# Attention and two mixtures on one core: quarter passes over the last keys put ahead of the values' full passes, and transfers of the later stages issued sooner

## The chip, the cores and the metric

One core of one Trainium2 chip runs the whole kernel. The metric is the device time of one launch in microseconds, and the comparison is between medians of runs of the kernel before and of the changed kernel on the same chip.

## The reference

Three layers follow each other; everything is float32. The first is attention over 4 batches, 12 heads, 448 rows and 64 columns, in which the scores are mixed over heads before the softmax and the weights after it. The second is a two-layer perceptron on 1792 tokens of 768 columns. The third is a mixture of 8 experts: a token whose skip score is positive goes through the one expert with the highest logit; the others pass unchanged.

```python
scores = np.einsum('bhij,hg->bgij', q @ k.transpose(0, 1, 3, 2) / 8, w_pre)
attn = softmax(scores)
x = (np.einsum('bhij,hg->bgij', attn, w_post) @ v)  # then 1792 x 768
h = x @ w_in                                        # 768 x 2048
x = np.where(h > 0, h, np.exp(np.minimum(h, 0)) - 1) @ w_out
e = argmax(x @ w_gate); prob = max(softmax(x @ w_gate))
out = x + (x @ w_skip > 0) * prob * (relu(x @ w1[e]) @ w2[e])
```

## The kernel before

**Attention.** The 16 row tiles (four to a batch: 120, 120, 120 and 88 rows) are taken in 48 units, three to a row tile. In the loop over units, TensorE gets for unit n: the mix over heads before the softmax (`mix_pre`, L205, 64x64 tiles), the mix over heads of the softmaxed weights of the unit before (`mix_post`, L265, 64x64 tiles, output `f`), the product with the values of an earlier tile (`av`, output `xp`), the scores of a later tile (`qk`, L164, 64x128 tiles), and the second `mix_post`. The values run over 448 keys as three full passes of 128 keys and a quarter pass of the 64 that remain: L286 are the full passes (twelve matmuls, seen as 24 passes in the trace), L293 the quarter passes (four, seen as eight). All of them accumulate in one PSUM tile: the first full pass opens it, the quarter pass closes it. Values start at unit 4. The scores of a unit belong five units ahead, so they end at unit 42; the last five units have products of the next stage between their parts. ScalarE and VectorE take the row maximum, the exponential and the copies out of PSUM, POOL makes the mixing matrices `kr`.

**Hidden products.** `products(s)` (L626) is the first matmul of the perceptron: 64 groups of 18 matmuls, 16 chunks of hidden columns times 4 batches. Weights arrive as 64-bit floats on SP's queue and are narrowed and split into two parts (high and low), and the activated result goes to DRAM as `gT`. `w_jobs` issues the loads and splits of one chunk. After the eighth group, `tables()` loads the router's weights (gate and skip, `wgt`, L583 and L584), turns the gate's columns on TensorE (`pt`, L589) and writes them as rows `wg` to DRAM. Up to the end of `tables` the order of instructions is as written; after it a scheduler orders each engine's instructions by due times. The second weight's chunks 0 to 8 are kept on chip, and 9 to 15 go to DRAM as `wf`.

**Second stage.** Fourteen row tiles of 128 tokens, 96 matmuls each (L899, output `o`): `load_g` reads `gT` back (`gr`) and splits it (`gh`), four quarters a tile. The seven chunks of `wf` are reloaded (`wr`, L845) through `raw0`, a pool of three buffers, and split into `w`; behind the last of them SP loads the router's rows for all partitions (`wrow`, L849, 3.46 MB). Each row tile is then scored on VectorE (L789, `junk`, nine to a tile), routed (`route`: maximum, exponential, one-hot `oh`) and seated (`seat`: a running count on TensorE gives each token its slot, which POOL scatters to `slots`). The last row tile's tokens are placed for expert 0 by TensorE (`place_old`).

**Experts.** Eight tiles of up to 128 tokens, and one more for the fullest expert. `load_w` brings weights in 0.79 MB pieces (`w1t`, 15 buffers), `part` splits them into `whi` and `wlo` (L1065, L1067), `gather` (L1072) fetches an expert's tokens by list from `x2d`, `turn` transposes them (L1082, output `pt`), `expert_first` and `expert_second` multiply. `plan` finds the fullest expert among the later ones; `reorder` (L1028 to L1038) swaps its list with the last expert's, from the table of lists `ids` and the mask `swap`, and writes `ordered`; gathers from expert 3 on use `ordered`. The order of a queue's entries is that in which they are issued, so a gather waits on POOL until its list is there.

Of the kernel before, what the change touches and what calls it, by code (L numbers as in the profile page):

```python
# [8 lines left out]
FP32 = mybir.dt.float32  # L9
# [4 lines left out]
ALU = mybir.AluOpType  # L14
# [4 lines left out]
B, H, S, D = 4, 12, 448, 64  # L19
NT, DM, DFF = B * S, H * D, 2048  # L20
NK = DM // 128
# [57 lines left out]
def attention(tc, q, k, v, w_pre, w_post, xT, mix):  # L79
# [12 lines left out]
    with ExitStack() as ctx, ExitStack() as mixing, ExitStack() as scoring:  # L92
# [181 lines left out]
        def av(T, u, ps=None):  # L274
# [7 lines left out]
            for i in range(2):  # L282
                p = 2 * u + i
                for jc in range(WHOLE):
                    for z in range(2):
                        nc.tensor.matmul(out=ps[i][z * 64:(z + 1) * 64, :n], lhsT=vt[b, p][:, jc * 2 + z, :],  # L286
                                         rhs=att[T][:, jc * H + ORDER.index(2 * p + z), :n], start=(jc == 0), stop=False)
            for i in range(2):
                p = 2 * u + i
                for z in range(2):  # L290
                    half = (z + p) % 2
                    keys = slice(half * JW, (half + 1) * JW)
                    nc.tensor.matmul(out=ps[i][z * 64:(z + 1) * 64, :n], lhsT=vt[b, p][keys, 2 * WHOLE, :],  # L293
                                     rhs=att[T][keys, WHOLE * H + p, :n], start=False, stop=True)
# [181 lines left out]
def mixtures(tc, order, xT, w_in, w_out, w_skip, w_gate, w1, w2, ident, gT, wf, wg, x2d, slots, out):  # L476
# [5 lines left out]
    with ExitStack() as top:  # L482
# [27 lines left out]
        with ExitStack() as ctx:  # L510
# [63 lines left out]
            def tables():  # L574
# [8 lines left out]
                nc.sync.dma_start(out=wgt[:, :, :E], in_=w_gate.rearrange("(k p) e -> p k e", p=128))  # L583
                nc.sync.dma_start(out=wgt[:, :, E], in_=w_skip.rearrange("(k p) -> p k", p=128))  # L584
# [127 lines left out]
            load_x(3)  # L712
            products(2)
# [31 lines left out]
        with ExitStack() as ctx:  # L745
# [47 lines left out]
            def route(i, lg):  # L793
# [3 lines left out]
                nc.vector.max_index(out=ix, in_max=mx, in_values=lg[:, :E])  # L797
                nmx = st_p.tile([128, 1], FP32, tag="nmx", name="nmx")
# [6 lines left out]
                ef = st_p.tile([128, 1], FP32, tag="ef", name="ef")  # L805
                nc.vector.tensor_copy(out=ef, in_=ix[:, 0:1])
                do = st_p.tile([128, 1], FP32, tag="do", name="do")
                nc.vector.tensor_scalar(out=do, in0=lg[:, E:E + 1], scalar1=0.0, scalar2=None, op0=ALU.is_gt)
                oh = st_p.tile([128, E], FP32, tag="oh", name="oh")
                nc.vector.tensor_scalar(out=oh, in0=iota8, scalar1=ef, scalar2=do, op0=ALU.is_equal, op1=ALU.mult)  # L810
# [32 lines left out]
            for fc in range(EARLY, NF):  # L843
                raw = raw0.tile([128, 2 * DM], FP32, tag="w", name="wr")[:, :DM]
                last_wr = nc.sync.dma_start(out=raw, in_=wf[fc - EARLY])  # L845
                wo[fc] = split(raw, ring_a if fc < RA + RB else ring2)
# [41 lines left out]
            for i, n, fc, cs in work:  # L888
# [35 lines left out]
                if fc == NF - 1:  # L924
                    if 0 in cs:
                        x2 = rows[i] = x2_p.tile([128, DM], FP32, tag="x2", name="x2")
                    for c in cs:
                        to, at = x2[:, cols[c]], po[c][:, :cols[c].stop - cols[c].start]
                        nc.scalar.copy(out=to, in_=at)  # L929
                        if last and c == 1:  # L930
                            turned, freed = score_turned(x2, c)
                            place_old(range(2))
                            logits(turned)
                            place_old(range(2, 5))
# [5 lines left out]
            place_old(range(5, NK))  # L940
# [9 lines left out]
        with ExitStack() as ctx:  # L950
# [284 lines left out]
            def jobs(*js):  # L1235

                return lambda *place: [f(*args) for at, f, *args in js if at == place]

            h, ht = new_h(), []
            expert_first([0], [h], jobs(((3, 2), turn_h, h, ht, 0)))  # L1240
            expert_second(0, ht, jobs(((0,), turn_h, h, ht, 1), ((2,), turn_x, 1)))
            h = new_h()
            expert_first([1], [h], jobs(((1, 2), turn_x, 2)))
            reorder()
            xg[3] = gather(ids[3])
# [111 lines left out]
```

## Time and profile before

| | |
|---|---|
| median of 3 runs | 1022.62 us (1020.44 to 1026.99) |
| the profiled execution | 1024.68 us |
| its span | 1022.9 us |
| TensorE busy in the span | 982.5 us (96%), 12226 matmuls |
| VectorE, ScalarE, POOL busy | 725.8, 555.9, 226.8 us |
| moved by DMA | 199.67 MB, mean 195 GB/s |
| mean granted TensorE clock | 0.988 |

Times in the rows are us from the start of the span. PE is the matmul side of TensorE, PEld its weight loads; "busy" of an engine leaves out instructions that only wait, branch or issue transfers. In a timeline a row is a run of like instructions: start, time up to the last one's end, engine, line, operation, output and inputs, shapes, count, and in brackets the idle time ahead of it with what ended it. In the waits, the numbers are the summed idle time, the count and the longest.

### The profile page before, as it was taken

What the parts mean: (1) busy time and instruction counts of PE and PEld (TensorE: products, weight loads), DVE (VectorE), ACT (ScalarE), POOL (GpSimd) and SP (SyncE); (2) the same over time, 40 slices, a digit from 0 to 9 for tenths busy, and PEclk for the clock granted to TensorE, in tenths of its full rate; (3) what the DMA queues carried; (4) which work ended last, traced back from release to release, by engine and by line L of the source; (5) the groups of instructions that cost most, each with busy time, mean ns of one, the idle gap of its engine ahead of it and who ended that gap; (6) DMA issues with size and microseconds to landing.
All of it is one profiled execution on the core that took longest, in us unless ns stands there. A gap on an engine that the chain in (4) does not pass through costs nothing. (4 is left out here: it accounts for less than half of the span.)

```text
span 1022.9 us, 30007 instructions
## 1 busy us (share of the span) xinstructions
PE 982.5 (96%) x12226; PEld 860.5 (84%) x12226; DVE 725.8 (71%) x1458; ACT 555.9 (54%) x1121; POOL 226.8 (22%) x295
## 2 busy tenths in 40 slices
PE   7899999999998899999999999999999999899997
PEld 4577777777766788999999999999999988799987
DVE  5677776777765777666666477777777748999963
ACT  5687787788765654445444462222222116788851
POOL 2233224224223312232332200010101003321002
PEclk9999999999998989999999999999999999999999
DMA  4665665675646565454665489543434396999800
GB/s 157 214 206 158 218 208 149 205 235 131 216 167 204 160 220 166 156 183 151 227 220 192 140 281 301 155 124 93 123 95 123 99 344 237 393 396 398 322 9 34
DMA packets 132297, 199.67 MB, mean 195 GB/s; under 512 B 35476, under 2 KB 99480, under 8 KB 131901
## 3 DMA queue, kind: packets, MB, share of 16 engines
q1 hardware_dynamic: 130013, 191.27, 56.4%
q0 software_dynamic: 2144, 6.46, 1.6%
q8 instruction: 97, 1.59, 0.7%
q14 instruction: 43, 0.35, 0.1%
HBM read 122.47 MB, written 37.65 MB: 157 GB/s over the span
## 5 line engine op out<-in xcount | busy, mean ns | idle before, releaser
L899 PE MATMUL o<-w,gh 128*128 128x384 f32 (+2 forms) x1344 | 239.2, 337 | 1.2 <-DVE w L505 0.8
L899 PEld LDWEIGHTS o<-w,gh 128*128 128x128 f32 x1344 | 231.9, 188 | 4.5 <-DVE w L505 1.4
L626 PE MATMUL h<-xh,w 128*128 128x448 f32 x1152 | 235.4, 367 | 0.0
L626 PEld LDWEIGHTS h<-xh,w 128*128 128x128 f32 x1152 | 217.4, 189 | 17.3 <-issue 0.4
L265 PEld LDWEIGHTS f<-kr,e 64*64 64x64 f32 x5888 | 106.3, 136 | 39.1 <-issue 29.5
L213 DVE TENSOR_REDUCE nmx<-c 128x1 f32<-128x448 f32 x184 | 102.4, 617 | 51.7 <-PE c L205 51.6
L226 ACT ACTIVATE e<-c,nmx 128x448 f32<-128x448 f32 x184 | 114.2, 632 | 23.0 <-DVE nmx L213 22.8
L789 DVE SCALAR_TENSOR_TENSOR junk<-x,wrow 128x768 f32<-128x768 f32 x117 | 111.8, 955 | 18.3 <-ACT x L929 12.8
L246 POOL TENSOR_SCALAR kr<-kpost,rs 128x60 f32<-128x60 f32 x184 | 78.4, 448 | 200.1 <-DVE rs L241 110.2
L1067 DVE TENSOR_TENSOR wlo<-w1t,whi 128x1536 fp32r<-128x1536 f32 x64 | 111.0, 1751 | 14.3 <-ACT whi L1065 14.0
L265 PE MATMUL f<-kr,e 64*64 64x60 f32 (+1 forms) x5888 | 108.4, 219 | 7.3 <-issue 3.5
L541 POOL TENSOR_TENSOR wf<-a,p 128x768 f32<-128x768 f32 x32 | 66.6, 2081 | 187.2 <-DVE p L539 139.5
L1065 ACT CAST whi<-w1t 128x1536 fp32r<-128x1536 f32 x64 | 93.9, 1482 | 20.6 <-PE ph L1094 9.4
L164 PE MATMUL qk<-k,qq 64*120 64x448 f32 (+1 forms) x576 | 82.6, 408 | 8.1 <-ACT k L135 4.5
L774 ACT CAST gh<-gr 128x512 fp32r<-128x512 f32 x56 | 35.0, 624 | 98.7 <-PE o L899 39.1
L205 PE MATMUL c<-d,kpre_low 64*64 64x448 f32 x368 | 83.3, 554 | 3.0 <-ACT s L168 2.8
L205 PE MATMUL c<-d,kpre_up 60*64 60x448 f32 x368 | 81.8, 554 | 0.0
L271 ACT COPY at<-f 128x420 f32<-128x420 f32 (+1 forms) x136 | 65.4, 516 | 28.2 <-PE f L265 27.2
L164 PEld LDWEIGHTS qk<-k,qq 64*120 64x120 f32 (+1 forms) x576 | 52.1, 186 | 27.8 <-issue 4.6
L286 PE MATMUL xp<-at,v 128*64 128x120 f32 (+1 forms) x1152 | 67.5, 266 | 7.3 <-issue 3.9
L168 ACT ACTIVATE s<-qk 120x448 f32<-120x448 f32 (+1 forms) x96 | 51.7, 544 | 35.5 <-PE qk L164 26.4
L169 DVE TENSOR_SCALAR s<-qk 120x448 f32<-120x448 f32 (+1 forms) x96 | 58.3, 621 | 16.1 <-PE qk L164 8.4
(180 smaller groups left out, 1255.7 us busy)
## 6 DMA issues: line engine op xcount, KB each, us to landing
w1t<-in_moe_w_dram SPq DMA_DIRECT2D x64, 768.0 KB
d<-s SPq DMA_DIRECT2D x176, 210.0 KB
gT<-g SPq DMA_DIRECT2D x64, 224.0 KB
f<-in_moe_w_in_dram SPq DMA_DIRECT2D x16, 768.0 KB
f<-in_moe_w_out_dram SPq DMA_DIRECT2D x16, 768.0 KB
gr<-gT SPq DMA_DIRECT2D x48, 256.0 KB
rk<-in_k_dram SPq DMA_DIRECT2D x24, 224.0 KB
v<-in_v_dram SPq DMA_DIRECT2D x24, 224.0 KB
```

Of the source, the lines that this page charges most:

```text
L164: nc.tensor.matmul(out=ps[:n, :S], lhsT=qt[T, p // 2][rows, a, p % 2, :n], rhs=kt[b, p][rows, z, :], start=(i == 0), stop=(i == 2))
L205: nc.tensor.matmul(out=ps[j * UP:(j + 1) * UP, :S], lhsT=kpre_up[UP:UP + HP, :] if z else kpre_low, rhs=d[z, j])
L213: nc.vector.tensor_reduce(out=t, in_=c, op=ALU.max, axis=AX.X, negate=True)
L226: nc.scalar.activation(out=e, in_=c, func=ACTF.Exp, bias=t, accum_out=sms[0][:, k + i:k + i + 1])
L246: nc.gpsimd.tensor_scalar(out=kr, in0=kposts[z], scalar1=rs[:, 2 * i + z:2 * i + z + 1], scalar2=None, op0=ALU.mult)
L265: nc.tensor.matmul(out=ps[to, heads, z, :], lhsT=e[rows, keys * JW:(keys + 1) * JW], rhs=kr[rows, first * HR:(first + n) * HR])
L286: nc.tensor.matmul(out=ps[i][z * 64:(z + 1) * 64, :n], lhsT=vt[b, p][:, jc * 2 + z, :], rhs=att[T][:, jc * H + ORDER.index(2 * p + z), :n] ...
L626: nc.tensor.matmul(out=ps, lhsT=w[:, a, kk, :], rhs=xs[tb, kk][:, z, :], start=(kk == 0 and a + z == 0), stop=(kk == NK - 1 and a == 1))
L789: nc.vector.scalar_tensor_tensor(out=t[:, o:o + n], in0=x2, scalar=1.0, in1=w, op0=ALU.mult, op1=ALU.mult, accum_out=lg[:, e:e + 1])
L899: mm = nc.tensor.matmul(out=po[c][:, :cols[c].stop - cols[c].start], lhsT=gs[i][fc // GC][:, a, fc % GC, :], rhs=wo[fc][:, z, cols[c]], st ...
L1065: nc.scalar.copy(out=hi, in_=t)
L1067: nc.vector.tensor_tensor(out=lo, in0=t, in1=hi, op=ALU.subtract)
```

## The change

1. `av`: the quarter passes come first and open the accumulation, the full passes follow and close it.
2. The two loads of `wgt` move out of `tables` to just behind the load of the fourth batch's `x`.
3. `route`: the cast of the index, the comparison of the skip score and the one-hot `oh` come ahead of the exponential, its sum and the reciprocal.
4. The reloads of `wf` share `raw0`'s buffers by twos: both loads of a pair are issued, then both are split.
5. `place_old` is split 2:4 and 4:6, where it was 2:5 and 5:6.
6. `reorder` and the gather of expert 3 come ahead of the second product of expert 0, where they came behind the first product of expert 1.

```diff
@@ av
-                for jc in range(WHOLE):
-                    for z in range(2):
-                        nc.tensor.matmul(out=ps[i][z * 64:(z + 1) * 64, :n], lhsT=vt[b, p][:, jc * 2 + z, :],
-                                         rhs=att[T][:, jc * H + ORDER.index(2 * p + z), :n], start=(jc == 0), stop=False)
-            for i in range(2):
-                p = 2 * u + i
                 for z in range(2):
                     half = (z + p) % 2
                     keys = slice(half * JW, (half + 1) * JW)
                     nc.tensor.matmul(out=ps[i][z * 64:(z + 1) * 64, :n], lhsT=vt[b, p][keys, 2 * WHOLE, :],
-                                     rhs=att[T][keys, WHOLE * H + p, :n], start=False, stop=True)
+                                     rhs=att[T][keys, WHOLE * H + p, :n], start=True, stop=False)
+            for i in range(2):
+                p = 2 * u + i
+                for jc in range(WHOLE):
+                    for z in range(2):
+                        nc.tensor.matmul(out=ps[i][z * 64:(z + 1) * 64, :n], lhsT=vt[b, p][:, jc * 2 + z, :],
+                                         rhs=att[T][:, jc * H + ORDER.index(2 * p + z), :n], start=False,
+                                         stop=(jc == WHOLE - 1))
@@ tables
-                nc.sync.dma_start(out=wgt[:, :, :E], in_=w_gate.rearrange("(k p) e -> p k e", p=128))
-                nc.sync.dma_start(out=wgt[:, :, E], in_=w_skip.rearrange("(k p) -> p k", p=128))
@@ ahead of products(2)
             load_x(3)
+            nc.sync.dma_start(out=wgt[:, :, :E], in_=w_gate.rearrange("(k p) e -> p k e", p=128))
+            nc.sync.dma_start(out=wgt[:, :, E], in_=w_skip.rearrange("(k p) -> p k", p=128))
             products(2)
@@ route
                 nc.vector.max_index(out=ix, in_max=mx, in_values=lg[:, :E])
+                ef = st_p.tile([128, 1], FP32, tag="ef", name="ef")
+                nc.vector.tensor_copy(out=ef, in_=ix[:, 0:1])
+                do = st_p.tile([128, 1], FP32, tag="do", name="do")
+                nc.vector.tensor_scalar(out=do, in0=lg[:, E:E + 1], scalar1=0.0, scalar2=None, op0=ALU.is_gt)
+                oh = st_p.tile([128, E], FP32, tag="oh", name="oh")
+                nc.vector.tensor_scalar(out=oh, in0=iota8, scalar1=ef, scalar2=do, op0=ALU.is_equal, op1=ALU.mult)
                 nmx = st_p.tile([128, 1], FP32, tag="nmx", name="nmx")
...
                 nc.vector.reciprocal(out=pairs[:, i, 1:2].bitcast(FP32), in_=sm)
-                ef = st_p.tile([128, 1], FP32, tag="ef", name="ef")
-                nc.vector.tensor_copy(out=ef, in_=ix[:, 0:1])
-                do = st_p.tile([128, 1], FP32, tag="do", name="do")
-                nc.vector.tensor_scalar(out=do, in0=lg[:, E:E + 1], scalar1=0.0, scalar2=None, op0=ALU.is_gt)
-                oh = st_p.tile([128, E], FP32, tag="oh", name="oh")
-                nc.vector.tensor_scalar(out=oh, in0=iota8, scalar1=ef, scalar2=do, op0=ALU.is_equal, op1=ALU.mult)
@@ reloads
-            for fc in range(EARLY, NF):
-                raw = raw0.tile([128, 2 * DM], FP32, tag="w", name="wr")[:, :DM]
-                last_wr = nc.sync.dma_start(out=raw, in_=wf[fc - EARLY])
-                wo[fc] = split(raw, ring_a if fc < RA + RB else ring2)
+            for f0 in range(EARLY, NF, 2):
+                raw = raw0.tile([128, 2, DM], FP32, tag="w", name="wr")
+                fcs = range(f0, min(f0 + 2, NF))
+                for fc in fcs:
+                    last_wr = nc.sync.dma_start(out=raw[:, fc - f0], in_=wf[fc - EARLY])
+                for fc in fcs:
+                    wo[fc] = split(raw[:, fc - f0], ring_a if fc < RA + RB else ring2)
@@ last row tile
-                            place_old(range(2, 5))
+                            place_old(range(2, 4))
...
-            place_old(range(5, NK))
+            place_old(range(4, NK))
@@ experts
             expert_first([0], [h], jobs(((3, 2), turn_h, h, ht, 0)))
+            reorder()
+            xg[3] = gather(ids[3])
             expert_second(0, ht, jobs(((0,), turn_h, h, ht, 1), ((2,), turn_x, 1)))
             h = new_h()
             expert_first([1], [h], jobs(((1, 2), turn_x, 2)))
-            reorder()
-            xg[3] = gather(ids[3])
```

On TensorE, a unit of attention stands like this before (`f` is the mix over heads, `xp` the values, `qk` the scores), with the mix ahead and the next mix behind:

```order
L265 MATMUL f<-kr,e 64x12x5 x12
L265 MATMUL f<-kr,e 64x6x5 x4
L286 MATMUL xp<-at,v 64x120 x12
L293 MATMUL xp<-at,v 64x120 x4
L164 MATMUL qk<-k,qq 120x448 x12
L265 MATMUL f<-kr,e 64x12x5 x12
```

and like this in the changed kernel, where L287 are the quarter passes and L293 the full ones:

```order
L265 MATMUL f<-kr,e 64x12x5 x12
L265 MATMUL f<-kr,e 64x6x5 x4
L287 MATMUL xp<-at,v 64x120 x4
L293 MATMUL xp<-at,v 64x120 x12
L164 MATMUL qk<-k,qq 120x448 x12
L265 MATMUL f<-kr,e 64x12x5 x12
```

The four quarter passes now stand between the mix and the twelve full passes; nothing else of the unit moved.

On SP's queue, at the end of the hidden products, the reloads (`wr`), reads of `gT` (`gr`) and the router's rows (`wrow`) stand like this before:

```order
L845 DMA wr<-wf_79 128x768
L771 DMA gr<-gT_0_61 128x4x128
L771 DMA gr<-gT_0_65 128x4x128
L637 DMA gT_3_76<-g 128x448
L771 DMA gr<-gT_0_69 128x4x128
L845 DMA wr<-wf_80 128x768
L771 DMA gr<-gT_0_73 128x4x128
L771 DMA gr<-gT_0_61 128x4x128
L845 DMA wr<-wf_81 128x768
L845 DMA wr<-wf_82 128x768
L845 DMA wr<-wf_83 128x768
L849 DMA wrow<-wg 128x3840
```

and like this in the changed kernel:

```order
L848 DMA wr<-wf_79 128x768
L848 DMA wr<-wf_80 128x768
L636 DMA gT_3_76<-g 128x448
L848 DMA wr<-wf_81 128x768
L848 DMA wr<-wf_82 128x768
L772 DMA gr<-gT_0_61 128x4x128
L772 DMA gr<-gT_0_65 128x4x128
L848 DMA wr<-wf_83 128x768
L853 DMA wrow<-wg 128x3840
L853 DMA wrow<-wg 128x3072
L772 DMA gr<-gT_0_69 128x4x128
L772 DMA gr<-gT_0_73 128x4x128
```

The reloads 80 to 83 moved ahead of reads of `gT` for the second row tile, and the router's rows ahead of two of these reads.

On VectorE, in the same place, the low halves of reloaded weights (`w`), of `gh` and the scorings of the first row tile (`junk`) stand like this before:

```order
L775 TENSOR_TENSOR gh<-gr,gh 128x512 x2
L505 TENSOR_TENSOR w<-wr,w 128x768 x2
L775 TENSOR_TENSOR gh<-gr,gh 128x512
L505 TENSOR_TENSOR w<-wr,w 128x768
L775 TENSOR_TENSOR gh<-gr,gh 128x512
L505 TENSOR_TENSOR w<-wr,w 128x768 x2
L775 TENSOR_TENSOR gh<-gr,gh 128x512
L505 TENSOR_TENSOR w<-wr,w 128x768
L789 SCALAR_TENSOR_TENSOR junk,lg<-x_10298,wrow 128x768 x9
L775 TENSOR_TENSOR gh<-gr,gh 128x512
```

and like this in the changed kernel:

```order
L506 TENSOR_TENSOR w<-wr,w 128x768 x5
L776 TENSOR_TENSOR gh<-gr,gh 128x512 x2
L506 TENSOR_TENSOR w<-wr,w 128x768
L790 SCALAR_TENSOR_TENSOR junk,lg<-x_10295,wrow 128x768 x6
L776 TENSOR_TENSOR gh<-gr,gh 128x512 x2
L790 SCALAR_TENSOR_TENSOR junk,lg<-x_10295,wrow 128x768 x3
L776 TENSOR_TENSOR gh<-gr,gh 128x512 x3
```

The third and fourth quarter of the second row tile's `gh` moved behind six of the first row tile's scorings.

Elsewhere, TensorE's transposes of `wgt` stand behind 126 of the products that follow the first group, where they stood behind 175, and POOL issues two gathers from `ordered` ahead of the first scatter of results, where it issued none.

## Rows read from the trace of the kernel before

**Rows 1.** Windows by stage: engines' busy time (instructions), granted clock, DMA share, GB/s

```profile
50.00:348.00 298.00, 286.63 (x8002) 217.54 (x7996) 208.91 (x471) 228.56 (x607) 93.57 (x187) 0.98 0.61 189
225.00:250.00 25.00, 24.59 (x697) 18.77 (x692) 18.49 (x42) 21.98 (x59) 13.22 (x22) 1.00 0.58 161
362.00:596.00 234.00, 231.81 (x1146) 214.52 (x1147) 155.86 (x224) 112.36 (x185) 61.34 (x30) 0.99 0.55 184
844.00:847.00 3.00, 3.00 (x16) 3.00 (x16) 0.69 (x6) 0.00 (x0) 0.68 (x1) 0.50 0.06 20
920.00:940.00 20.00, 20.00 (x112) 18.20 (x111) 19.57 (x17) 16.42 (x17) 4.58 (x3) 1.00 1.04 398
```

**Rows 2.** Waits of PE over the whole span

```profile
PE pt L1082 <- DMA xg<-x2d,ordered: 3.0, 1, 3.0
...
PE pt L589 <- DMA wgt<-in_moe_w_gate_dram: 2.2, 1, 2.2
```

**Rows 3.** Timeline of PE, one unit of attention (start, duration, instruction)

```profile
150.68 1.08 PE L265 MATMUL f<-kr,e 64*64 64x60 f32 x64
151.69 1.45 PE L286 MATMUL xp<-at,v 128*64 128x120 f32 x24
153.07 0.44 PE L293 MATMUL xp<-at,v 64*64 64x120 f32 x8
153.44 1.48 PE L164 MATMUL qk<-k,qq 64*120 64x448 f32 x12
154.84 1.13 PE L265 MATMUL f<-kr,e 64*64 64x60 f32 x64
155.79 0.57 PE L205 MATMUL c<-d,kpre_low 64*64 64x448 f32 x1
```

**Rows 4.** Timeline of PE, two later units without scores

```profile
345.65 0.43 PE L293 MATMUL xp<-at,v 64*64 64x120 f32 x8
345.90 1.08 PE L265 MATMUL f<-kr,e 64*64 64x60 f32 x64
...
355.26 0.38 PE L293 MATMUL xp<-at,v 64*64 64x88 f32 x8
355.57 1.13 PE L286 MATMUL xp<-at,v 128*64 128x88 f32 x24
```

**Rows 5.** Timeline of PE, hidden products up to the router's transposes

```profile
362.38 37.21 PE L626 MATMUL h<-xh,w 128*128 128x448 f32 x175
...
401.78 0.82 PE L589 MATMUL pt<-ident,wgt 128*8 128x128 f32 x6 [2.19 <-DMA wgt<-in_moe_w_gate_dram]
```

**Rows 6.** Timeline of SP's queue, the fourth batch's x

```profile
370.18 2.77 SPq L552 DMA_DIRECT2D xr<-xT  x6
```

**Rows 7.** Timeline of PE, first row tile of the second stage and after

```profile
596.46 13.77 PE L899 MATMUL o<-w,gh 128*128 128x384 f32 x78
...
611.46 2.01 PE L899 MATMUL o<-w,gh 128*128 128x384 f32 x10 [0.38 <-DVE w L505]
...
614.63 17.67 PE L899 MATMUL o<-w,gh 128*128 128x384 f32 x100 [0.38 <-DVE w L505]
```

**Rows 8.** Timeline of SP's queue, last reloads and the router's rows

```profile
605.87 2.66 SPq L845 DMA_DIRECT2D wr<-wf  x3
608.63 0.85 SPq L849 DMA_DIRECT2D wrow<-wg  x2
```

**Rows 9.** Timeline of DVE, first scoring

```profile
617.55 0.96 DVE L789 SCALAR_TENSOR_TENSOR junk<-x,wrow 128x768 f32<-128x768 f32 x1 [2.98 <-DMA wrow<-wg]
```

**Rows 10.** Timeline of POOL, gather of expert 3

```profile
881.48 2.25 POOL L1072 DMA_INDIRECT xg<-x2d,ordered  x1 [6.36 <-DVE ordered L1035]
```

**Rows 11.** Timeline of DVE, the mask for the swap, and splits of weights

```profile
861.92 0.15 DVE L981 TENSOR_SCALAR swap<-star 128x8 int32<-128x8 f32 x1
...
884.37 3.41 DVE L1067 TENSOR_TENSOR wlo<-w1t,whi 128x1536 fp32r<-128x1536 f32 x2
```

**Rows 12.** Timeline of PE, transposes of expert 3

```profile
889.73 0.30 PE L1082 MATMUL pt<-ident,xg 128*128 128x128 f32 x1 [3.02 <-DMA xg<-x2d,ordered]
```

## The prediction

> **What bounds the kernel now.** The page comes first. TensorE is busy 982.5 us of a span of 1022.9, so the time is TensorE's own work plus its short waits, and an edit elsewhere pays only where TensorE waits for it. The windows by stage [rows 1] say how firm that is: in attention (50 to 348) TensorE is busy 286.63 of 298 us, in the stage of hidden products (362 to 596) 231.81 of 234. Attention leaves little slack beside it: in the stretch where keys are also split (225 to 250) ScalarE works 21.98 of 25 us. In the experts (920 to 940) VectorE works 19.57 of 20 and the DMA engines are full.
>
> The waits of TensorE name what ends its pauses. Two entries are transfers that come late [rows 2]: 3.0 us for the gathered rows of an expert and 2.2 us for the router's weights. Pauses smaller than a microsecond don't show there. For them I read TensorE's timeline: once inside a unit of attention [rows 3, 4], then at the three places that the change touches later [rows 5, 7, 12]. Behind each stood one look at the queue that brings the late data [rows 6, 8, 10] and at VectorE's work beside it [rows 9, 11].
>
> **Part 1: quarter passes lead (attention).** No matmul is added or removed. What changes is which shapes meet. Before, a unit goes mix (64x64 tiles), full passes (128x64), quarter passes (64x64), scores (64x128), mix: three changes of tile shape up to the scores. After it, mix and quarter passes have one shape, so two changes are left, quarter to full and full to scores. What one costs I read from starts [rows 3, 4]. The quarter passes take 153.44 - 153.07 = 0.37 us up to the scores, but 345.90 - 345.65 = 0.25 us up to a mix of their own shape: 0.12 for the change. A mix takes 151.69 - 150.68 = 1.01 us up to full passes and 155.79 - 154.84 = 0.95 up to the 64x64 product after it: 0.06. I take the middle, 0.09. It counts where scores follow the values. Values start at unit 4, and scores are five units ahead, so they end at unit 42: 39 units. 39 x 0.09 = 3.5 us; by the ends 2.3 and 4.7, and 0 if another engine sets the pace. In the other nine units a mix or more values follow: the shapes change as often as before, so nothing there.
>
> The Trainium skill (page "TensorEngine Tiling (Array Packing)", section "Key Properties") says that changing the tiling mode, not merely the tile, drains TensorE; the two start distances above agree. Its page "TensorE: Matmul & The Clock Gate", section "Step-by-step: what each phase is for", gives about 128 cycles for the last column to leave the array, 53 ns at 2.4 GHz; an estimate by that page would be 39 x 0.053 = 2.1 us instead of 3.5.
>
> **Part 2: router weights loaded early.** Before, their six transposes stand behind 175 products, and the data is 2.19 us late [rows 5]. The change issues the load right behind that of the fourth batch's x; that one's six issues end at 370.18 + 2.77 = 372.95 [rows 6]. The transposes now stand behind 126 products, so they want the data at 362.38 + 126 x 37.21/175 = 389.2. That leaves 16 us, so the whole 2.2 goes. SP issues two more transfers ahead of the next weight load, so that one starts about 1 us later (SP spends 2.66/3 = 0.9 us on a wr issue [rows 8]); it is narrowed only when the products of the next chunk are under way, and TensorE has its products queued. Ends: 0 and 2.2.
>
> **Part 3: reloads in pairs.** The first row tile of the second stage waits for reloaded weights. By 614.63 it has done 78 + 2 + 10 + 2 = 92 of its 96 matmuls [rows 7]. At the steady 17.67/100 = 0.1767 us the 92 would have ended at 596.46 + 92 x 0.1767 = 612.72: 1.9 us lost, in pieces that end with VectorE's or ScalarE's split. Three reloads fit in three buffers; in pairs six do, and the seventh waits for two splits. So the whole loss goes. The router rows (wrow), issued at 608.63 behind the last reload [rows 8], come with it some 4 us sooner, and were wanted at 617.55 by the first scoring, which waited 2.98 for them [rows 9].
>
> What is late next: the order on VectorE now puts six scorings ahead of the split of tile 1's third quarter. Tile 0 would end at 612.72 + 4 x 0.1767 = 613.4; about 1.2 later its rows are copied out; six scorings at 0.96 [rows 9] bring 620.4, and the split (0.8) 621.2. TensorE wants it 48 matmuls into tile 1: 613.4 + 48 x 0.1767 = 621.9. Just in time. If the router rows landed no sooner than before, it would be 617.55 + 5.8 + 0.8 = 624.1, 2.2 us late. I take +1.9; ends: -0.3 and +1.9.
>
> **Part 4: the swapped list and its gather sooner.** TensorE waits 3.02 us at expert 3's transposes, up to 889.73 [rows 12]. The gather that it waits for was issued at 881.48, the queue having stood 6.36 us for the list `ordered` [rows 10]: 8.2 us from issue to use. One input of `ordered`, `swap`, was there at 861.92 [rows 11]; the other is the table of lists, whose transfer POOL issues behind the gathers of experts 0 to 2; no row here dates its landing, and I take it to be in by then. After the change the list comes right behind both, near 863, and the gather near 865, landing at about 873, against a want at 889.73 - 3.02 = 886.7. POOL's only other work in the way is the gather itself, now ahead of the first scatter of results, which nobody reads. VectorE meets the small reorder operations ahead of splits of weights; these wait for nothing late if the table has landed. What is late next is a split of weights (1.71 us each): VectorE ends one at 884.37 + 3.41/2 = 886.1 [rows 11], 0.6 before the want, the second at 887.8. If TensorE wants that one within the same microsecond, up to 1.5 us comes back as a wait for it. Ends 1.5 and 3.0; I take 3.0, since the transposes want no weights.
>
> **Part 5: the router's order, and placing 2:4 and 4:6.** Three small VectorE operations move ahead of the exponential, and two of TensorE's placing matmuls move behind the last seat. At the end of the stage TensorE is busy 3.00 of 3.00 us [rows 1], at a granted clock of 0.50, the lower of its two levels (1.2 of 2.4 GHz), after the products thinned out there. A filled stretch has nothing to give: 0, with 0.3 either way.
>
> **Sum.** 3.5 + 2.2 + 1.9 + 3.0 = 10.6. The profiled execution took 1024.68 us (its span and 1.8 around it): 1014.1. It lies 2.06 above the median of the three runs, 1022.62, and inside them (1020.44 to 1026.99). Against the median the sum gives 1012.0.
>
> **Rivals.** *Attention is paced elsewhere.* If ScalarE (21.98 of 25 us) or a fixed chain from mix to copy sets the unit, the 3.5 stay as idle time: 1015.5. For it: ScalarE's share where keys are split. Against: TensorE is busy 24.59 of the same 25.
>
> *The experts are bound by transfers or VectorE.* Then the 3.0 come back as later waits for weights: 1015.0. For it: 398 GB/s and VectorE 19.57 of 20 [rows 1]. Against: TensorE is busy 20.00 of the same 20.
>
> *Tile 1 waits behind the scorings.* Part 3 turns from +1.9 into -0.3: 1014.2.
>
> *Slower: the new meeting costs more than the old.* If going from quarter to full passes, now with the accumulation begun by the small tile, stalled TensorE in all 48 units, it would eat parts 2 to 4 (7.1) from 7.1/48 = 0.15 us per unit, and be over 1% slower from (7.1 + 10.2)/48 = 0.36. At 0.4 it takes 19.2: 1022.6 - 7.1 + 19.2 = 1034.7. Against: at 355.26 quarter passes of one group already meet full ones of the next, 0.31 from start to start [rows 4]; with 88 of 120 columns 0.25 shrinks to 0.18, so that change costs 0.13, no more than the others. For it: there the next accumulators are other ones.
>
> *Nothing arrives:* the waits are replaced one for one, 1022.
>
> **Chances.** Two medians of this kernel differ by chance up to about 1%, 10.2 us; below 1012.4 counts as faster. Forecast (own range 1009 to 1014.5, about three in four of it below 1012.4): 0.56. Attention paced elsewhere 0.17, experts 0.12, tile 1 0.07, all three within 1%; some of the first ends faster if parts 2 to 4 give their ends. Slower 0.04. Nothing 0.04. That makes faster 0.45, same 0.51, slower 0.04. The range: all upper ends (4.7 + 2.2 + 1.9 + 3.0 + 0.3 = 12.1) give 1010.5, less half the runs' spread (3.3) 1007; attention lost, part 3 at its lower end and part 4 at its own leave 2.2 - 0.3 + 1.5 = 3.4, so 1019.2, rounded up to 1020.
>
> **What would show it.** TensorE's timeline in attention: mix to quarter near 0.95, quarter to full near 0.37, full to scores unchanged or 0.05 longer, and the attention stage some 3.5 us shorter. No wait of TensorE for wgt; its transposes at about 386 to 389. Tile 0's 96 matmuls in 17 us and no pause at 48 of tile 1. No wait for xg in the experts, the gather issued before 870. Wrong would be a stage of attention as long as before, a wait of 1 us or more for gh near 620, or new waits for whi or wlo behind 887.

## The result and the profile after

| | before | changed |
|---|---|---|
| median (runs) | 1023.41 us (4: 1020.44 to 1026.99) | 1013.55 us (4: 1006.87 to 1017.75) |
| ratio to before | | 0.9879, 95% interval 0.983 to 0.9929 |
| profiled execution, its span | 1024.68, 1022.9 us | 1017.75, 1016.0 us |
| TensorE busy, mean granted clock | 982.5 us, 0.988 | 978.6 us, 0.984 |

By the medians the change gained 9.9 us, 1.0%; the ratio in the table, 0.9879, is 1.2% or 12.4 us. The forecast was 1012.0, with 10.6 us of gain. The line of 1% at which the chances were drawn runs between the two.

The waits of TensorE in the changed kernel, longest sums first (engine and tile, what it waited for: sum in us, times, longest):

```profile
PE f L265 <- issue: 5.1, 6, 2.0
PE qk L164 <- ACT k L135: 4.9, 1, 4.9
PE f L265 <- DVE at L271: 3.4, 1, 3.4
PE xp L293 <- issue: 3.0, 4, 1.2
PE xp L287 <- DVE x L303: 2.9, 1, 2.9
PE c L205 <- ACT s L168: 2.8, 1, 2.8
```

Both entries of [rows 2], for `xg` and for `wgt`, are gone from the list. What is left stands in attention. A pause that ends with "issue" is one in which TensorE waited for nothing that the profile shows. The windows of the same stretches as [rows 1]:

```profile
50.00:348.00 298.00, 282.87 (x8030) 214.97 (x8024) 208.85 (x472) 228.18 (x606) 94.57 (x189) 0.98 0.61 189
362.00:596.00 234.00, 233.95 (x1163) 216.66 (x1160) 157.50 (x225) 113.17 (x187) 63.09 (x30) 0.99 0.57 186
920.00:940.00 20.00, 20.00 (x110) 18.42 (x109) 18.58 (x16) 16.04 (x15) 3.59 (x2) 1.00 1.04 398
```

The hidden products are now filled (233.95 of 234). Attention is not: TensorE was busy 3.8 us less in the same 298 us, and the stage took no less time. That was the first thing to explain. Cut at three starts of TensorE (first hidden product, first `o`, first `ph`, the hidden product of an expert), the two profiles compare like this:

| stage | before | changed |
|---|---|---|
| start to the first hidden product | 348.66 | 349.27 |
| to the first matmul of the second stage | 247.80 | 245.60 |
| to the first product of expert 0 | 252.45 | 250.06 |
| to the end of the span | 173.99 | 171.07 |

The three later stages give 2.2 + 2.4 + 2.9 = 7.5 us, all that the spans differ by and more. Attention, where 3.5 was forecast, gave -0.6. Yet inside a unit the gain is plain. TensorE's timeline of a unit, to be laid beside [rows 3]:

```profile
140.24 1.08 PE L265 MATMUL f<-kr,e 64*64 64x60 f32 x64
141.14 0.42 PE L287 MATMUL xp<-at,v 64*64 64x120 f32 x8
141.49 1.45 PE L293 MATMUL xp<-at,v 128*64 128x120 f32 x24
142.87 1.44 PE L164 MATMUL qk<-k,qq 64*88 64x448 f32 x12
144.23 1.13 PE L265 MATMUL f<-kr,e 64*64 64x60 f32 x64
```

From the mix to the values it is 0.90 us (1.01 before), quarter to full 0.35 (0.37 before up to the scores), full to scores 1.38 as before. In other units the trace shows the last mixing passes and the first quarter passes interleaved:

```profile
194.79 0.80 PE L265 MATMUL f<-kr,e 64*64 64x60 f32 x41
195.40 0.28 PE L287 MATMUL xp<-at,v 64*64 64x88 f32 x1
195.42 0.27 PE L265 MATMUL f<-kr,e 64*64 64x30 f32 x6
195.51 0.36 PE L287 MATMUL xp<-at,v 64*64 64x88 f32 x7
```

So 0.13 us per unit, 39 x 0.13 = 5.1 us. What hid it in this profile are pauses of TensorE that end with "issue" and stretches at the lower clock level. Between 48 and 300 us the changed kernel's profile has nine such pauses, 8.2 us in all (before: four, 5.1), the longest this one:

```profile
126.75 0.26 PE L265 MATMUL f<-kr,e 64*64 64x30 f32 x5 [1.99 <-issue]
```

Its granted clock fell to 0.50 twice before 300 us (first near 36, then after the pause above), that of before only once, near 294. The columns are those of [rows 1]:

```profile
36.00:38.00 2.00, 1.92 (x9) 1.12 (x13) 1.15 (x2) 1.57 (x5) 0.00 (x0) 0.50 0.85 259
128.00:130.00 2.00, 2.00 (x22) 1.68 (x20) 0.34 (x1) 0.00 (x0) 1.65 (x4) 0.50 0.32 118
```

So the pauses are 3.1 us longer in sum, and the stretches at the lower level some 7 us longer, which at half the clock is up to 3.4 us of time. By this estimate 6.5 us stood against the 5.1, enough for a stage that is 0.6 longer. But one profile of each kernel can't show that it is always so. The experiments had to.

### The profile page after: what moved, and what is told of

It reads as the page before. It is cut to its first block, busy times and chain, and to the rows that moved or that the text cites. A ratio compares the mean times of both kernels' runs of the same rounds, so it can differ in the third digit from the quotient of the medians.

```text
span 1016.0 us, 30002 instructions
## 1 busy us (share of the span) xinstructions
PE 978.6 (96%) x12226; PEld 860.0 (85%) x12226; DVE 724.7 (71%) x1458; ACT 555.6 (55%) x1121; POOL 244.6 (24%) x295
## 5 line engine op out<-in xcount | busy, mean ns | idle before, releaser
L164 PEld LDWEIGHTS qk<-k,qq 64*120 64x120 f32 (+1 forms) x576 | 52.6, 187 | 26.3 <-ACT k L135 4.9
L293 PE MATMUL xp<-at,v 128*64 128x120 f32 (+1 forms) x1152 | 68.8, 268 | 3.0 <-issue 3.0
```

What stands on the lines that cost most here:

```text
L164: nc.tensor.matmul(out=ps[:n, :S], lhsT=qt[T, p // 2][rows, a, p % 2, :n], rhs=kt[b, p][rows, z, :], start=(i == 0), stop=(i == 2))
```

## The experiments

**The order of the values, alone and taken back.** Four kernels on one chip, beside 23 runs of the kernel before (median 1024.06). The first is the changed kernel again.

> The changed kernel once more, with a second profile. Theory: all four terms are there in every execution, so about 9.9 us below the kernel before (ratio 0.990), and the trace shows the same stages after attention as the first profile (hidden products 245.6 us, second stage with the move to the experts 250.1, experts 171.1, each within 0.3). Attention differs from profile to profile: the first one had 8.2 us of pauses of TensorE that end with issue (between 48 and 300 us) and two stretches at the lower clock, the kernel before 5.1 us and one. Rival: the new order of the values itself makes more such pauses; then this profile shows about 8 us again.

Measured: 1012.66 us (6 runs), ratio 0.9887, interval 0.9854 to 0.9921. Attention was 7 us shorter than in the first profile (first hidden product at 342.24), with 4.1 us of pauses before 300 us and no fall of the clock before 316. The later stages took 246.7, 249.2 and 170.7, none of them within the 0.3 that I had expected. So the first profile's attention was one draw among several; the rival on more pauses is taken up below.

In the second kernel only the order in `av` is as before:

```diff
-                                     rhs=att[T][keys, WHOLE * H + p, :n], start=True, stop=False)
-            for i in range(2):
-                p = 2 * u + i
                 for jc in range(WHOLE):
...
+                                         rhs=att[T][:, jc * H + ORDER.index(2 * p + z), :n], start=(jc == 0), stop=False)
+            for i in range(2):
+                p = 2 * u + i
                 for z in range(2):
...
+                                     rhs=att[T][keys, WHOLE * H + p, :n], start=False, stop=True)
```

> The changed kernel with the values' full passes leading again, as before. Theory (a change of tile shape costs TensorE 0.1 us or a little more, nothing else paces attention): 39 units times 0.13 us (start distances of the two profiles) = 5.1 us more than the changed kernel. My own term before the result was 3.5. Rival (attention paced by ScalarE or by the supply of instructions): within 1.5 us of the changed kernel. In the trace: 1.02 us from a mix to the full passes, no mix interleaved with values.

Measured: 1015.51 us (6 runs), ratio 0.9916, interval 0.9886 to 0.9947: 2.9 us above the changed kernel. The two intervals overlap, so these times alone don't exclude the rival. Its trace shows the old distances, 1.03 from mix to values and 0.36 from quarter to scores:

```profile
143.03 1.10 PE L265 MATMUL f<-kr,e 64*64 64x60 f32 x64
144.06 1.45 PE L286 MATMUL xp<-at,v 128*64 128x120 f32 x24
145.44 0.44 PE L293 MATMUL xp<-at,v 64*64 64x120 f32 x8
145.80 1.46 PE L164 MATMUL qk<-k,qq 64*88 64x448 f32 x12
```

Unit by unit against the changed kernel's second profile, the start of the scores comes 0.1 to 0.15 us later with each undisturbed unit; the pauses add or take away 0.4 to 2.4 us at a time. The unit itself is a constant of the order: from the mix to the scores its median is 2.76 us in both profiles with the old one and 2.63 in each of the eleven with the new one. Of the 0.13, 0.11 lies between the mix and the values. The third kernel is the one before with the new order in `av` and nothing else.

> The kernel before with the order of the values alone changed. Theory: 5.1 us faster than before (ratio 0.995), the later stages as before (hidden products 247.8 us with 2.2 us of waiting for the router's weights, experts 174.0). Rival (attention paced elsewhere): within 1.5 us of before.

Measured: 1019.8 us (12 runs), ratio 0.9951, interval 0.9923 to 0.9979: 5.0 us by the ratio, 4.3 by the medians. Hidden products 248.2, experts 175.3, with the old waits for `wgt` (1.86) and `xg`. The interval is 2.1 to 7.9 us of gain, so the order alone makes the kernel faster; the two estimates are 2.9 and 5.0. "Attention paced elsewhere" (within 1.5) falls. The fourth kernel meets more changes of shape:

```diff
                                      rhs=att[T][keys, WHOLE * H + p, :n], start=True, stop=False)
-            for i in range(2):
-                p = 2 * u + i
                 for jc in range(WHOLE):
```

> The changed kernel with quarter and full passes alternating by pair of heads: quarter, full, quarter, full, so four changes of tile shape where it has two up to the scores. The work is the same. Theory (each change costs 0.11 to 0.13 us of TensorE's time): 48 units times 2 more changes times 0.12 = 11.5 us more than the changed kernel, so slower than before by 1 to 2 us. Rival (the gain came from the mix running together with the quarter passes, and the other changes cost nothing): within 2 us of the changed kernel. Rival (attention paced elsewhere): within 2 us as well, with TensorE's pauses smaller.

Measured: 1025.75 us (12 runs), ratio 1.0024, interval 0.9998 to 1.0049: 13.1 above the changed kernel, near the 11.5 that the theory asked for, but by luck: the units grew by twice as much, and about half of it arrived. The unit:

```profile
140.68 0.42 PE L287 MATMUL xp<-at,v 64*64 64x120 f32 x4
141.03 0.84 PE L291 MATMUL xp<-at,v 128*64 128x120 f32 x12
141.79 0.42 PE L287 MATMUL xp<-at,v 64*64 64x120 f32 x4
142.15 0.84 PE L291 MATMUL xp<-at,v 128*64 128x120 f32 x12
142.91 1.44 PE L164 MATMUL qk<-k,qq 64*88 64x448 f32 x12
```

Four quarter passes take the 0.35 us that eight took: for the same columns the two pairs of heads use different halves of the rows, and they had run side by side. A unit's values grew by 0.50 us (2.23 from the first quarter pass to the scores, 1.73 in the changed kernel). The full passes, which this does not touch, give a clean price: 24 in one run took 1.38 us up to the scores, two runs of 12 take 0.76 each, so one change more costs 0.14. The rival in which the other changes cost nothing falls by this reading, not by the time. The other 0.36 is the second group of quarter passes, an estimated 0.25 of passes that no longer run together ([rows 4]: 0.25 without a change of shape) and 0.11 for a change. And 48 x 0.50 = 24 us of longer units came out as 13.1 in the median: some 0.55 of what the units show. For the new order it is 2.9 to 5.0 of 5.1. In this profile the pauses before 300 us sum to 2.6 us, in the two with the old order to 5.1 and 4.0, in the eleven with the new order to 4.1 to 8.2, 5.8 in the mean. One place shows how some of the gain can go. At the 4779th matmul the mix runs through before the change, and it stops in the changed kernel's second profile:

```profile
204.34 1.08 PE L265 MATMUL f<-kr,e 64*64 64x60 f32 x64
```

```profile
200.99 0.59 PE L265 MATMUL f<-kr,e 64*64 64x60 f32 x27
202.55 0.70 PE L265 MATMUL f<-kr,e 64*64 64x30 f32 x33 [0.97 <-issue]
```

It stops there in ten of the eleven profiles with the new order (0.2 to 2.3 us, 1.0 in the mean of all eleven) and in none of the three others; a second place (the 3639th) stops in nine of eleven, 0.4 in the mean, and in none of the three. That shorter units meet longer pauses fits the part that is missing; with three profiles on one side it is not shown.

**The four other parts, each taken back.** On another chip, beside 23 runs of before (median 1022.93). All four are the changed kernel with one part as before. The changed kernel itself did not run beside them, and the interval of each reaches into that of the changed kernel above (0.9854 to 0.9921), so what a part is worth is read from the traces.

```diff
             load_x(3)
-            nc.sync.dma_start(out=wgt[:, :, :E], in_=w_gate.rearrange("(k p) e -> p k e", p=128))
-            nc.sync.dma_start(out=wgt[:, :, E], in_=w_skip.rearrange("(k p) -> p k", p=128))
...
                 nc.sync.dma_start(out=x2d[NT:NT + 1, :], in_=wgs[0:1, :])
+                nc.sync.dma_start(out=wgt[:, :, :E], in_=w_gate.rearrange("(k p) e -> p k e", p=128))
+                nc.sync.dma_start(out=wgt[:, :, E], in_=w_skip.rearrange("(k p) -> p k", p=128))
```

> The changed kernel with the two loads of the router's weights back in the tables. Theory: TensorE's transposes (after 175 products again) wait 2.2 us for the data, and the kernel takes 2.2 us more than the changed one. Rival (the load was hidden by another delay that remains): no wait for wgt, the same time within 1 us.

Measured: 1014.73 us (10 runs), ratio 0.9913, interval 0.9884 to 0.9943. The wait is back, but smaller than before:

```profile
400.40 0.82 PE L590 MATMUL pt<-ident,wgt 128*8 128x128 f32 x6 [0.73 <-DMA wgt<-in_moe_w_gate_dram]
```

Counted from the first hidden product, the data came 0.7 us sooner than in [rows 5] (400.40 - 348.02 = 52.4, there 401.78 - 348.66 = 53.1), and TensorE wanted it 0.7 later (51.7 and 50.9). The expected 2.2 was a miss in size. With the 1.86 of the kernel above, this part is worth 0.7 to 2.2.

```diff
-            for f0 in range(EARLY, NF, 2):
-                raw = raw0.tile([128, 2, DM], FP32, tag="w", name="wr")
...
+            for fc in range(EARLY, NF):
+                raw = raw0.tile([128, 2 * DM], FP32, tag="w", name="wr")[:, :DM]
+                last_wr = nc.sync.dma_start(out=raw, in_=wf[fc - EARLY])
+                wo[fc] = split(raw, ring_a if fc < RA + RB else ring2)
```

> The changed kernel with one reload to a buffer again, three in flight. Theory: four short pauses of TensorE before w in the first row tile, 1.2 us of idle shown and 2.2 us from the first to the 192nd matmul lost against the changed kernel (35.7 us instead of 33.4). Rival (six in flight are not what helps, the earlier router rows are): the first row tile without pauses, and pauses at the second instead. Rival (the loads are sooner anyway because attention ends sooner): nothing lost.

Measured: 1011.95 us (8 runs), ratio 0.9903, interval 0.9872 to 0.9935. In the trace the first row tile stops again for `w`:

```profile
608.28 2.62 PE L900 MATMUL o<-w,gh 128*128 128x384 f32 x12 [0.37 <-DVE w L506]
611.28 17.66 PE L900 MATMUL o<-w,gh 128*128 128x384 f32 x100 [0.37 <-DVE w L506]
```

The two first row tiles took 35.4 us; eleven profiles with reloads in pairs show 33.4 to 34.6. So 0.8 to 2.0 lost, though the timed runs don't show it.

```diff
-            reorder()
-            xg[3] = gather(ids[3])
             expert_second(0, ht, jobs(((0,), turn_h, h, ht, 1), ((2,), turn_x, 1)))
             h = new_h()
             expert_first([1], [h], jobs(((1, 2), turn_x, 2)))
+            reorder()
+            xg[3] = gather(ids[3])
```

> The changed kernel with the reorder and the gather of expert 3 back behind the first product of expert 1. Theory: the gather is issued some 32 us after the seat of the last tile, TensorE waits 3.0 us for it at its first transpose of expert 3, and the experts take 2.9 us more (174.0 instead of 171.1 from the first hidden product of expert 0 to the end). Rival (weights paced the experts anyway): the wait is there, but the time to the end is the same within 0.5 us.

Measured: 1015.29 us (10 runs), ratio 0.9936, interval 0.9905 to 0.9966; the experts took 173.9 us, and the wait of [rows 12] is back whole:

```profile
880.11 0.30 PE L1086 MATMUL pt<-ident,xg 128*128 128x128 f32 x1 [3.26 <-DMA xg<-x2d,ordered]
```

That the weights pace the experts falls: they took 2.8 us longer than in the changed kernel's first profile.

```diff
-                ef = st_p.tile([128, 1], FP32, tag="ef", name="ef")
...
                 nc.vector.reciprocal(out=pairs[:, i, 1:2].bitcast(FP32), in_=sm)
+                ef = st_p.tile([128, 1], FP32, tag="ef", name="ef")
...
-                            place_old(range(2, 4))
+                            place_old(range(2, 5))
```

> The changed kernel with the router's order and the split of the placing matmuls (2:5, 5:6) as before. Theory (this part was worth 0, at most 0.3): from the last six matmuls of the row tiles to expert 0's first product 9.6 us instead of 9.5, total time unchanged within the runs' spread. Rival (this end of the stage is a chain through the one-hot, and its order pays): 0.6 us or more longer.

Measured: 1012.55 us (5 runs), ratio 0.9887, interval 0.9831 to 0.9942. From the last six matmuls of the row tiles (836.55) to expert 0's first product (846.03) it took 9.48 us; in the changed kernel 844.93 - 835.46 = 9.47. Both had the lower clock for some of that time; under it, this part of the change is worth nothing.

**What the profiles offered next.** Two waits of the list above stand at the end of attention in every profile so far: 3.4 us for `at` and 2.9 for `x`. In the changed kernel's timeline of TensorE:

```profile
326.64 0.44 PE L265 MATMUL f<-kr,e 64*64 64x60 f32 x2 [3.38 <-DVE at L271]
...
360.57 0.57 PE L287 MATMUL xp<-at,v 64*64 64x88 f32 x8 [2.91 <-DVE x L303]
```

and the reason for the first, on VectorE, which stands for the first weight's transfer ahead of the next maximum:

```profile
323.30 0.56 DVE L533 TENSOR_SCALAR a<-a 128x768 int32<-128x768 int32 x1 [6.46 <-ACT a L530]
```

Both were moved, together and alone. (a) is the first piece below: a `yield` is a place in attention's units, and the narrowing begins at the sixth instead of the third, with its later steps closed up. (b) is the second.

```diff
             raws[0] = load_w_in(0)
             yield
             yield
             yield
-            step = narrowing(raws.pop(0))
-            next(step)
             yield
             load_x(0)
             yield
-            next(step)
             yield
+            step = narrowing(raws.pop(0))
             next(step)
...
-        next(mix)
         moves = [av(len(tiles) - 1, 0), av(len(tiles) - 1, 1, [ps_f.tile([128, 512], FP32, tag="f", name="xp") for _ in range(2)])]
         moves[0]()
         moves.append(av(len(tiles) - 1, 2))
-        for f in moves[1:]:
-            f()
+        moves[1]()
+        next(mix)
+        moves[2]()
```

> The changed kernel with two more moves, at waits that every profile here shows at the end of attention, with the old order of the values and with the new. (a) The narrowing of the first weight, whose transfer is issued at 314.66 and lands at 322.3, comes two units' parts later, so that ScalarE and VectorE don't stand for it (3.6 and 6.5 us) in front of the next softmax; TensorE waits 3.4 us behind that, and its clock is at the lower level for some 7 us right after. (b) The last values are copied out of PSUM ahead of the splits of the second batch's x; TensorE waits 2.9 us for that copy, and the lower clock follows for some 6 us. No arithmetic is changed. Theory: both waits go (6.3 us), and with them a part of the stretches at the lower clock (up to 3 us each): 6 to 12 us below the changed kernel, 1001 to 1007. Rival (attention's end is bound by the transfer of the weights or by x): the waits move to the first hidden products, and the time stays within 2 us.

> Move (a) alone. Theory: 3.4 us of waiting for `at` and up to 3 us of lower clock behind it go: 3 to 6 us below the changed kernel, and the second wait (2.9 for x) stays. Rival: the first hidden products wait for their weights instead, nothing gained.

> Move (b) alone. Theory: 2.9 us of waiting for x and up to 3 us of lower clock go: 3 to 6 us below the changed kernel, and the first wait (3.2 to 3.7 for `at`) stays. Rival: the products of the second batch wait for their split x instead, nothing gained.

Measured beside 11 runs of before (median 1021.13): both 0.989 (0.9846 to 0.9933), (a) alone 1011.19 us and 0.988 (0.9845 to 0.9916), (b) alone 1013.95 us and 0.9909 (0.9875 to 0.9944). All three lie where the changed kernel lies, so my 6 to 12 us for both is refuted by these runs. (Both ran six times; one execution took 4211.67 us, for a reason that the record does not show, and is not in the ratio.) The waits themselves went; of the first, 0.6 to 1.3 us are left with (a). With both moves, the last values of attention run through (compare the 2.91 above):

```profile
351.84 0.38 PE L287 MATMUL xp<-at,v 64*64 64x88 f32 x8
352.16 1.13 PE L293 MATMUL xp<-at,v 128*64 128x88 f32 x24
353.22 4.18 PE L625 MATMUL h<-xh,w 128*128 128x448 f32 x19
357.65 10.59 PE L625 MATMUL h<-xh,w 128*128 128x448 f32 x50 [0.26 <-DVE xh L561]
```

From the last scores (307.85) to these products it is 45.4 us; the ten profiles without these moves have 52.0 to 54.0, (a) alone 52.6, (b) alone 49.3. To learn whether the timed runs had been unlucky, both moves ran once more.

> Both late moves once more. Its first profile shows the end of attention (last scores to the products of the second batch) in 45.4 us, where ten kernels without the moves show 52.0 to 54.0, yet its timed runs lay no lower than those of the changed kernel (ratio 0.989 as against 0.988 and 0.989). Theory: the 7 us are there in every execution, and the five runs were slow by chance in the stretch before (units 4 to 42 took 254.3 us in its profile, 249.8 to 255.6 in others of the same order): ratio 0.982 to 0.985, tail again 45 to 46.5. Rival (the time comes back behind attention, where the hidden products wait or the clock falls instead): ratio 0.988 to 0.990, and a later stage longer by some 5 us than in the changed kernel.

Measured beside 11 other runs of before (median 1023.95): 1009.58 us (6 runs), ratio 0.987, interval 0.984 to 0.990. Between the two expectations, and they are not told apart. Its profile took 49.2 us over the same stretch, because of a pause that the first profile with both moves did not have, with the lower clock behind it:

```profile
340.40 1.67 PE L293 MATMUL xp<-at,v 128*64 128x120 f32 x23 [2.67 <-issue]
```

The profile of (a) alone has the same pause at the same matmul, where the ten profiles without the moves show at most 0.6:

```profile
336.96 2.66 PE L293 MATMUL xp<-at,v 128*64 128x120 f32 x23 [2.46 <-issue]
```

So in two of the three profiles with (a), some 2 us of the 3.4 that it took away came back as a pause that waits for no data, and (a) alone left the end of attention at 52.6. Only (b), 49.3, shortened it by itself. In the second profile with both moves the later stages were no longer than in the changed kernel (242.9, 249.0, 170.7), so the rival of a return behind attention falls too. By its two ratios (0.989, 0.987) this version lies within 2 us of the changed kernel (0.988, 0.989), on either side. Whether it beats it stays open.

## Why the prediction was right, point by point

The time (1012.0 against 1013.55) and the sum (10.6 against 9.9 by the medians, 12.4 by the ratio) came out; the terms did so unevenly.

**Part 1, 3.5 us.** The mechanism is right: with the order alone the kernel gains 2.9 to 5.0, and a changed shape costs 0.11 to 0.14 us. The size per unit was too small: 0.13, not 0.09. I had averaged 0.12 and 0.06, and the 0.06 (a mix up to full passes against a mix up to the next product) was the wrong measure, since quarter passes start while the mix still drains, 0.05 sooner than the product that I took for the mark. The estimate by the Trainium skill's page "TensorE: Matmul & The Clock Gate" (section "Step-by-step: what each phase is for": some 128 cycles, 2.1 us in all) was lower still; the measured 0.11 to 0.14 per change decides. That the term nevertheless fits is luck: it was a third too small for the unit, and not all of the 5.1 reached the end.

What I said would show it was "the attention stage some 3.5 us shorter". In the profile that came with the result it was 0.6 longer. The mark was badly chosen: a sum over 300 us of a stage with pauses and falls of the clock. The distances inside a unit, which I named as well, were the mark that held.

**Part 2, 2.2 us.** The load was issued at 373.57, as worked out (373), and no wait is left:

```profile
373.57 0.43 SPq L712 DMA_DIRECT2D wgt<-in_moe_w_gate_dram  x1
```

The transposes stood at 390.07, a microsecond past the 389 named. The hidden products are 2.2 us shorter, and not by chance alone: in the seven profiles with the early load (those with late moves aside) they take 244.2 to 246.7, 245.3 in the mean, in the three with the old load 247.0 to 248.2, 247.7 in the mean. Other profiles have the wait at 1.9 and 0.7, so 2.2 was the upper end of what it is worth.

**Part 3, 1.9 us.** The 192 matmuls of two row tiles took 628.30 - 594.87 = 33.43 us, before 632.13 - 596.46 [rows 7] = 35.67: 2.2. The changed kernel without a pause, and the end of the 192 before the change:

```profile
594.87 33.59 PE L903 MATMUL o<-w,gh 128*128 128x384 f32 x192
628.30 0.28 PE L818 MATMUL pp<-seen,ones 128*128 128x8 f32 x2
```

```profile
632.13 0.28 PE L817 MATMUL pp<-seen,ones 128*128 128x8 f32 x2
```

"Just in time" for the third quarter of tile 1 was right to a few tenths. VectorE's timeline, beside [rows 9]:

```profile
613.21 0.96 DVE L790 SCALAR_TENSOR_TENSOR junk<-x,wrow 128x768 f32<-128x768 f32 x1 [3.96 <-DMA wrow<-wg]
...
619.10 1.29 DVE L776 TENSOR_TENSOR gh<-gr,gh 128x512 fp32r<-128x512 f32 x2
```

The third quarter is split by 619.10 + 0.65 = 619.75, and TensorE wants it 48 matmuls into tile 1, at 594.87 + 144 x 33.43/192 = 619.94. In the changed kernel's second profile it came too late:

```profile
615.35 7.93 PE L903 MATMUL o<-w,gh 128*128 128x384 f32 x44 [0.41 <-DVE gh L776]
```

So the rival of tile 1 is real. Of the eleven profiles with reloads in pairs, six take 33.43 and five 0.2 to 1.1 us more (0.8 here, 1.1 where the wait was 0.85): in the worst half of the gain, never the whole. "No pause at 48 of tile 1" held in about half of the executions.

**Part 4, 3.0 us.** The swapped list stood at 857, and the gather was issued at once:

```profile
857.05 0.95 POOL L1076 DMA_INDIRECT xg<-x2d,ordered  x1 [2.81 <-DVE swapped L1040]
```

That is 4 us earlier than my 865, after the 4.0 us by which the stage began sooner (844.93 for 848.91) are taken off. The wait is gone, no wait for `whi` or `wlo` took its place, and the experts took 2.9 us less.

**Part 5, 0.** 9.47 and 9.48 us with and without it, both with a fall of the clock; without one it was not compared.

**The rivals.** Attention paced elsewhere: fallen as a cause, though part of the gain is lost on the way. Experts bound by transfers: fallen. Slower by the new meeting of shapes: fallen, quarter to full costs no more than the others.

## What to carry to other kernels

Where matmuls of several tile shapes alternate on TensorE, put those of one shape next to each other, and measure what a change costs as a distance between starts, in a unit with and one without it. A gain of 0.13 us per unit is certain in the timeline long before it is visible in a stage or a total; a stage's length in one profile says nothing below its own spread (here 6 us), and one has to add up waits that are named, or take the part back on the same chip. A wait taken away where the next cause stands close behind it (here, it seems, the pauses that end with "issue") may give back only a share.

## What the runs showed of the hardware that was not expected

**Pauses with no data to wait for.** TensorE's pauses that end with "issue" stand at the same places of the program in all profiles, though not every place stops in each, and their length is drawn anew: near 125 us 0.3 to 2.0 us (none in one profile), near 165 to 171 us 0.7 to 2.1. Between 48 and 300 us they sum to between 2.6 and 8.2 us. The places follow a count: of the 129 such pauses over 0.15 us in the fourteen profiles, from 20 us to the first hidden product, any two stand a multiple of 256 TensorE instructions apart, to within one (matmuls, weight loads and waits counted together; some 127 matmuls). TensorE's pauses for data in the same stretch do not keep to these places. That points to how instructions reach the engine; what happens at every 256th the traces don't tell. Beside the clock they are what the traces show of the spread from run to run, and no run here changed them on purpose.

**The lower clock as a lottery.** Ahead of expert 0 the granted clock fell to 0.50 in nine of the fourteen profiles and not in others of the same kernel. The same place in the changed kernel's two profiles:

```profile
842.00:844.00 2.00, 2.00 (x11) 2.00 (x11) 0.11 (x1) 0.00 (x0) 0.72 (x1) 0.50 0.00 0
```

```profile
836.00:838.00 2.00, 2.00 (x20) 2.00 (x19) 0.67 (x5) 0.41 (x1) 0.44 (x1) 1.00 0.01 0
```

From the last six row-tile matmuls to expert 0 it took 9.47 us in the first and 838.12 - 830.28 = 7.84 in the second: 1.6 us, about what part 2 or part 3 is worth. The other profiles fall on the same two sides: 9.35 to 9.80 in the nine with the fall, 7.84 or 7.85 in the five without.
